# Attention and routed experts on one core: a planner's tie rule, where the row maxima are written, and the attention's end cut in parts

## The chip, the cores and the metric

The kernel runs on one core of one Trainium2 chip. The metric is the device time of one execution in microseconds (us): 815.42 us as the median of three runs before the change (815.18 to 823.71). One further execution was recorded by the profiler; it took 812.64 us.

## The reference

Eight batch elements with eight heads, 576 positions and head size 64. Attention has a causal mask and a bias from running sums, and its output goes, token by token, to one of eight experts with a capacity of 576 tokens each.

```python
scores = 1/sqrt(D) * q @ k.T
bias = -(cum[:, :, :, None] - cum[:, :, None, :])        # cum = cumsum(max(s, 0))
scores = where(causal, -1e9, scores + minimum(bias, 0))
attn = exp(scores - max(scores)); attn = attn / (sum(attn) + 1e-9)
x = (attn @ v) as [4608 tokens, 512]
logits = x @ w_gate                                      # [4608, 8]
for idx in argsort(-logits.flatten()):                   # best pair first
    tok, e = idx // 8, idx % 8
    if assigned[tok] < 0 and counts[e] < 576: assigned[tok] = e; counts[e] += 1
out[mask_e] = max(x[mask_e] @ w1[e], 0) @ w2[e]          # for each expert e
```

## The kernel before

**Two stages.** The attention (class `Attention`) writes x, split in two f16 halves, to a DRAM tensor `xs` and the logits to a tile `L`. Then `route_and_experts` finds the experts' tokens in eight phases (class `Router`) and runs the experts one after the other (class `Moe`): gather by token numbers, first product, relu, second product, scatter. Nearly all products are made from f16 parts (high and low), hence the many matmuls.

**A planner sets the order.** The kernel is scheduled by hand: `Plan.add` takes a task with its engine (t = PE, a = ACT, v = DVE, p = POOL, s = SP's DMA queue), an estimated duration, what it depends on, a priority, and the ring buffers that it uses. `Plan.run` simulates the engines when the kernel is built. In each step it takes for each engine the task that can start first (by priority among equals) and starts the one of these that can start earliest; equal times are decided by priority. The instructions are emitted in that order. On the chip each engine's queue is in order, so the plan decides what stands behind what; semaphores do the rest. A task with `lock=True` on DVE or POOL starts in the plan only when the other engine's last locked task is over: this is how the plan models the port to SBUF that DVE and POOL share. All of POOL's compute tasks are locked. A task with `alt` may go to a second engine.

**The attention.** One group g is half the heads of a batch element (16 groups), one pass is a pair of heads (two per group, 32 in all, n = 2g + pr). Per pass:

- `load` and `vload` (once per group) fetch q, k and v; ACT makes the high parts (L379, L412), DVE the low parts (L381 for q and k, L414 for v: `Vl`); SP moves halves between partitions (L386).
- `spass`: PE computes score tiles into one of three PSUM buffers `pss` (L473, L457), and DVE takes each row's maximum with one fused instruction, mask added (`tri`, L442). It writes its elementwise result to a buffer `scr`, of which there is one and which nobody reads, and the maximum to a column of `mr`. Ten of these per pass. The maxima are turned (L489 to L497) and go by DMA into rows of QK (L499, `mt`).
- `sts`: PE computes the transposed scores with the maximum subtracted into `pst` (L514 to L517, L556 to L558), ACT takes the exponential into P (L525), POOL subtracts P's bfloat16 high part from it (L527): R. Six R of 512 columns and one of 128 per pass.
- `pv`: three matmuls per tile pair into `po` (L587 to L589), five query tiles per head. `norm` divides by the row sum on DVE (L602 to L604), makes the high half of x on ACT (L606) and the low half on DVE (L608).
- `turn`: PE transposes the two halves (L635), ACT copies them to `xt` (L638), PE computes the logits' dots with `wgp` (L645), which `gate` made from w_gate (L304, L306). After a batch element DVE adds them up into L (L651).

After the fourth, seventh and eighth batch element `batch_tasks` runs `choose` (L815 to L827, eleven small DVE instructions: best expert, its key, its digit) on the columns that are new. `xout` writes x to `xs` at the end of each batch element (L616, L618).

**The router's first phase** compares the digits of all 40 columns with all thresholds (L906, `ge`), counts by matmul (L929, L939), and narrows in seven such steps. Its pools are opened after the attention's pools are closed and lie in the same memory.

## Time and profile before

| what | us |
|---|---|
| median of three runs | 815.42 |
| the profiled execution | 812.64 |
| its span on the core | 810.9 |
| PE busy, of the span | 726.9 (90%) |
| DVE busy | 607.9 (75%) |
| ACT busy | 379.6 (47%) |
| POOL busy | 345.6 (43%) |

PE is the matmul unit, PEld its weight load, DVE the vector engine, ACT the scalar engine, POOL GpSimd, SP the queue that issues most DMAs. L442 is line 442 of the kernel. A row of the timeline has the start and the duration in us, engine, line, operation, written and read tiles with their shapes, and in brackets how long the engine had been idle and for whom it waited. Matmul rows are pipelined: their starts are what counts. Shares over the whole span say little here, since the attention (to about 318 us), its tail, the first phase of the router (to about 395 us) and the experts have different limits.

### The profile page before, as it was taken

To read this page: it belongs to the slowest core of one execution; us is meant where nothing else is said; L and a number is where in the kernel's file an instruction comes from. 1 tells how busy PE (TensorE), PEld (TensorE's weight loads), DVE (VectorE), ACT (ScalarE), POOL (GpSimd) and SP (SyncE) were. 2 spreads that over 40 slices of the span, in tenths; PEclk is the share of its full clock that TensorE was granted. 3 is DMA by queue.
4 is the path that set the end of the run, shared out by engine and by line. 5 is a ranking of instruction groups with operands and counts; after the bars stand their busy time and mean duration, and the time that the engine had idled before them with its cause. 6 is when DMAs were issued, how large, how long until landed. Compare 5 with 4: busy or idle time off the path is not lost.

```text
span 810.9 us, 22772 instructions
## 1 busy us (share of the span) xinstructions
PE 726.9 (90%) x8814; PEld 459.3 (57%) x8814; DVE 607.9 (75%) x2070; ACT 379.6 (47%) x724; POOL 345.6 (43%) x425
## 2 busy tenths in 40 slices
PE   4188999999999999824899999999999999999995
PEld 1066788878778888712754545545445454454542
DVE  8768999999999997658888887887878888350110
ACT  3356788878778776602532333432234333341110
POOL 4268788787879887601105031130222114301111
PEclk8578999999999999955999999999999999999998
DMA  4956567686847431013438265393837548931001
GB/s 125 315 163 168 161 196 212 168 238 162 255 135 228 110 102 62 2 59 125 144 118 234 90 162 165 132 232 132 150 124 202 156 143 196 280 117 39 21 21 38
DMA packets 85315, 119.27 MB, mean 147 GB/s; under 512 B 40726, under 2 KB 57238, under 8 KB 85206
## 3 DMA queue, kind: packets, MB, share of 16 engines
q1 hardware_dynamic: 79318, 98.93, 43.3%
q0 software_dynamic: 5888, 18.88, 7.7%
q8 instruction: 69, 1.13, 0.6%
q14 instruction: 40, 0.33, 0.1%
HBM read 71.67 MB, written 19.10 MB: 112 GB/s over the span
## 4 chain that ended last, share of the span: by engine, by line
PE 58%; issue 18%; DVE 12%; DMA 5%; POOL 4%; SPq 1%; ACT 1%; POOLq 0%; another core or an unknown queue 0%; DVEq 0%; ACTq 0%
PE psm L1200 14%; PE psm L1274 13%; DVE scr L442 5%; PE pst L515 4%; PE pst L514 4%; PE pss L473 3%; PE po L587 3%; PE po L589 2%; PE po L588 2%; PE psm L1271 2%; PE psn L1204 2%; POOL out_dram L1254 2%; PE pss L635 1%; PE pss L457 1%; POOL xg L1134 1%
## 5 line engine op out<-in xcount | busy, mean ns | idle before, releaser
L527 POOL TENSOR_TENSOR R<-P 128x512 f16<-128x512 f32 (+1 forms) x224 | 232.8, 1066 | 50.8 <-ACT P L525 49.9
L1200 PE MATMUL psm<-xT,w1p 128*128 128x512 f16 (+1 forms) x876 | 194.1, 353 | 0.0
L1274 PE MATMUL psm<-w2p,hT 128*128 128x512 f16 x768 | 174.7, 379 | 0.0
L525 ACT ACTIVATE P<-pst 128x512 f32<-128x512 f32 (+1 forms) x224 | 119.0, 548 | 50.5 <-PE pst L517 23.2
L1204 PE MATMUL psn<-xT,w1p 128*128 128x64 f16 x768 | 142.2, 193 | 0.0
L442 DVE CUSTOM_DVE_ANT_0 scr<-pss,mS 128x512 bf16<-128x512 f32 (+3 forms) x256 | 124.7, 487 | 16.0 <-PE pss L473 6.4
L1200 PEld LDWEIGHTS <-w1p 128*128 128x128 f16 x876 | 79.7, 98 | 81.6 <-issue 1.4
L1134 POOL DMA_INDIRECT xg<-xs,ids x40 | 42.9, 1072 | 191.7 <-DVE val L824 52.9
L1254 POOL DMA_INDIRECT out_dram<-y,ids x40 | 41.5, 1037 | 183.7 <-ACT y L1285 156.9
L587 PE MATMUL po<-V,P 128*128 128x65 f16 x960 | 113.7, 196 | 2.4 <-DVE xp L608 2.0
L514 PE MATMUL pst<-QK 70*128 70x64 f16 (+4 forms) x512 | 109.0, 252 | 6.8 <-DMA QK<-mt 6.8
L1274 PEld LDWEIGHTS <-hT 128*128 128x128 f16 x768 | 69.0, 98 | 80.4 <-issue 4.0
L589 PE MATMUL po<-V,R 128*128 128x65 f16 x960 | 113.7, 194 | 0.1
L588 PE MATMUL po<-Vl,P 128*128 128x64 f16 x960 | 113.4, 193 | 0.0
L515 PE MATMUL pst<-QK 128*128 128x64 f16 (+4 forms) x512 | 107.6, 251 | 0.0
L1220 ACT ACTIVATE hT<-psm 128x512 f16<-128x512 f32 x64 | 38.2, 597 | 123.5 <-PE psm L1200 103.0
L588 PEld LDWEIGHTS <-P 128*128 128x128 bf16 x960 | 89.9, 99 | 7.8 <-issue 2.8
L587 PEld LDWEIGHTS <-P 128*128 128x128 bf16 x960 | 90.3, 98 | 5.8 <-issue 2.3
L473 PE MATMUL pss<-QK 67*128 67x512 f16 (+3 forms) x256 | 74.1, 311 | 17.6 <-DVE mr L442 10.1
L589 PEld LDWEIGHTS <-R 128*128 128x128 f16 x960 | 89.8, 97 | 0.3 <-POOL R L527 0.3
L1285 ACT ACTIVATE y<-psm 128x512 f32<-128x512 f32 x32 | 19.1, 597 | 122.7 <-PE psm L1274 105.2
L1204 PEld LDWEIGHTS <-w1p 128*128 128x128 f16 x768 | 72.8, 98 | 0.6
(210 smaller groups left out, 1394.1 us busy)
## 6 DMA issues: line engine op xcount, KB each, us to landing
QK<-QK SPq DMA_DIRECT2D x120, 144.0 KB
wst<-in_w_dram SPq DMA_DIRECT2D x32, 512.0 KB
wst<-in_w_dram SPq DMA_DIRECT2D x64, 256.0 KB
rv<-in_v_dram SPq DMA_DIRECT2D x16, 576.0 KB
raw<-in_q_dram SPq DMA_DIRECT2D x15, 576.0 KB
raw<-in_k_dram SPq DMA_DIRECT2D x15, 576.0 KB
xs<-xp SPq DMA_DIRECT2D x8, 1024.0 KB
xs<-xp SPq DMA_DIRECT2D x8, 128.0 KB
```

The costliest lines, as they stand in the source:

```text
L442: return pl.add("v", dur, lambda: nc.vector.tensor_tensor_reduce(scr.t[:, :n], ps(), mask, 1.0, init() if init else -3e38, OP.add, OP.max, ...
L473: nc.tensor.matmul(ps.t[:, :n], F()[:, q0:q0 + 128], F()[:, k0:k0 + n], start=True, stop=True)
L514: nc.tensor.matmul(ps[:, c0:c0 + n], F()[:, ks:ks + 128], F()[:, q:q + n], start=True, stop=False)
L515: nc.tensor.matmul(ps[:, c0:c0 + n], G()[:, ks:ks + 128], G()[:, q:q + n], start=False, stop=not diag)
L525: e = pl.add("a", n / 1200 + 0.171, lambda: nc.scalar.activation(P.t[:, c0:c0 + n], ps.t[:, :n], AF.Exp, scale=1.0 / YS), [x] + fresh, pri ...
L527: sub = lambda eng: eng.tensor_tensor(R.t[:, c0:c0 + n], P.t[:, c0:c0 + n], strided_hi(P.t)[:, c0:c0 + n], op=OP.subtract)
L587: nc.tensor.matmul(o[:, i], H[:, c:c + 128], V.t[:, pr, sl], start=f, stop=False)
L588: nc.tensor.matmul(o[:, i, 0:64], H[:, c:c + 128], Vl.t[:, pr, sl], start=False, stop=False)
L589: nc.tensor.matmul(o[:, i], R.t[:, c:c + 128], V.t[:, pr, sl], start=False, stop=l)
L1200: nc.tensor.matmul(ps[:, tiles[0]:tiles[-1] + 1] if len(tiles) > 1 else ps[:, tiles[0]], lhs(f, c, a), xT.t[:, tiles[0]:tiles[-1] + 1, 4 * ...
L1204: nc.tensor.matmul(pt.t[:, 64 * f:64 * f + 64], lhs(f, c, a), xT.t[:, 4, 4 * b + c, 0:64], start=s, stop=e)
L1274: nc.tensor.matmul(py.t, hT.t[:, f, a, 128 * i:128 * i + 128], w2p.t[:, f, b], start=f == 0 and k == 0, stop=f == 7 and k == 2)
```

## The change

- **Tie rule.** In `Plan.run`, tasks of different engines that can start at the same time are now compared first by the time since which task and engine have been waiting, and only then by priority. Two tasks that wait for the shared port fall under this.
- **Maxima.** `tri` writes its elementwise result back to the PSUM buffer that it read; `scr` is gone.
- **Sooner.** The two pieces of `gate` get priority -20 (before: 1), the low part of v 2g - 2 (before: 2g - 0.9).
- **Locks.** Nine of the eleven pieces of `choose` are locked in the plan. The batch after the seventh element has its priority number raised by 5 where it was 2.
- **End of the attention.** R of the last pass may go to DVE. The norm of the last head pair is made in two parts, tiles 0 to 2 and 3 to 4 (`parts`), as are the turn, the copies (the second may go to DVE) and the dots.
- **Router.** The last batch element's logits are no longer added up in the attention but in the first phase (`late`), with `choose` on its five columns, between the first eight tenths of the first `ge` and the rest; one reduce replaces two. The three pools of the router are opened with `reuse_waits="tile"`: a tile waits for the tiles that lay in its place, where before all waited for the closing of the old pools.

```diff
-                if best is None or (t, x.prio, x.rank) < best[:3]:
-                    best = (t, x.prio, x.rank, x, e)
+
+                z = (t, max(x.ready, self.free[e]), x.prio, x.rank, x, e)
+                if best is None or z[:4] < best[:4]:
+                    best = z
             assert best is not None, "no task can go on"
-            self.start(best[0], best[3], best[4])
+            self.start(best[0], best[4], best[5])
...
-            mt=R(w, [20, 128], F16, "mt", 2), scr=R(w, [128, 512], BF, "scr", 1, False),
+            mt=R(w, [20, 128], F16, "mt", 2),
...
         x = pl.add("v", 0.2, lambda: nc.vector.tensor_scalar(self.wgp[:, :, 0, :], self.wgf, GS, None, op0=OP.mult), [ld],
-                   prio=1, lock=True)
+                   prio=-20, lock=True)
         self.k["gate"] = pl.add("v", 0.2, lambda: nc.vector.scalar_tensor_tensor(
-            self.wgp[:, :, 1, :], self.wgf, GS, self.wgp[:, :, 0, :], op0=OP.mult, op1=OP.subtract), [x], prio=1, lock=True)
+            self.wgp[:, :, 1, :], self.wgf, GS, self.wgp[:, :, 0, :], op0=OP.mult, op1=OP.subtract), [x], prio=-20, lock=True)
...
-            Vl.t, rv.t, VS, V.t[:, :, :, 0:64], op0=OP.mult, op1=OP.subtract), [hi], prio=t0 - 0.9, uses=[rv, V, Vl], lock=True)
+            Vl.t, rv.t, VS, V.t[:, :, :, 0:64], op0=OP.mult, op1=OP.subtract), [hi], prio=t0 - 2, uses=[rv, V, Vl], lock=True)
...
-            scr = self.buf("scr")
             dur = n / 960 + 0.156 + (0.06 if init else 0)
             return pl.add("v", dur, lambda: nc.vector.tensor_tensor_reduce(
-                scr.t[:, :n], ps(), mask, 1.0, init() if init else -3e38, OP.add, OP.max, mr.t[:, o:o + 1]),
-                [dep] + list(more), prio=prio, uses=[ps.buf, scr, mr])
+                ps(), ps(), mask, 1.0, init() if init else -3e38, OP.add, OP.max, mr.t[:, o:o + 1]),
+                [dep] + list(more), prio=prio, uses=[ps.buf, mr])
...
-            r = pl.add("p", n / 547 + 0.1, lambda: sub(nc.gpsimd), [e] + fresh, prio=prio + 0.3, uses=[P, R])
+            r = pl.add("p", n / 547 + 0.1, lambda: sub(nc.gpsimd), [e] + fresh, prio=prio + 0.3, uses=[P, R], lock=True,
+                       alt=("v", n / 960 + 0.16, lambda: sub(nc.vector)) if n0 == 4 * self.nb - 1 else None)
...
+                xs_[i] = x
+            for a, z in self.parts(n0, par):
+                self.norm(g, pr, par, po, den, xp, xs_[z - 1], a, z)
+
+    def parts(self, n, par):
+
+        return ((0, 3), (3, 5)) if n == 4 * self.nb - 1 and par else ((0, 5),)
...
+        m = z - a
+        o = lambda: po.t[:, 0:325].rearrange("p (i c) -> p i c", c=65)[:, a:z]
...
+        lo = V(0.157 + m / 15, lambda: v.tensor_sub(xp.t[:, a:z, 1, h:h + 64], o()[:, :, 0:64], xp.t[:, a:z, 0, h:h + 64]), [hi], us=[xp])
+        self.xdone.setdefault(b, []).append((hi, lo, a, z))
...
+        for i0, i1 in self.parts(2 * g + pr, 1):
+            m, out = i1 - i0, []
+            need = [f for f in fin if f[2] < i1 and f[3] > i0]
+            for a in range(2):
+                ps = self.buf("pss")
+
+                def turn(a=a, ps=ps, i0=i0, m=m):
+                    for i in range(m):
+                        nc.tensor.transpose(ps.t.bitcast(F16)[:, 128 * i:128 * i + 128],
+                                            xp.t[:, i0 + i, a, 128 * c:128 * c + 128], self.ident16)
+                x = pl.add("t", 0.058 * m, turn, [f[a] for f in need] + [k["i16b"]], prio=prio, uses=[ps, xp])
+                cp = lambda e, a=a, ps=ps, i0=i0, i1=i1, m=m: e(
+                    xt.t[:, a, i0:i1].rearrange("p i c -> p (i c)"), ps.t.bitcast(F16)[:, 0:128 * m])
+                last = 2 * g + pr == 4 * self.nb - 1 and a
+                out.append(pl.add("a", 0.171 + m * 0.1067, lambda cp=cp: cp(lambda y, z: nc.scalar.activation(y, z, AF.Copy)), [x],
+                                  prio=prio, uses=[ps, xt], alt=("v", 0.157 + m * 0.1333, lambda cp=cp: cp(nc.vector.tensor_copy)) if last else None))
+
+            def dots(i0=i0, i1=i1):
+                for i in range(i0, i1):
+                    for a, w in ((0, 0), (0, 1), (1, 0)):
+                        nc.tensor.matmul(o[:, c, i], xt.t[:, a, i], self.wgp[:, c, w], start=(a, w) == (0, 0), stop=a == 1)
+            x = self.dots = pl.add("t", 0.088 * m, dots, out + [k["gate"], self.dots] + free, prio=prio + 0.5, uses=[xt])
...
+        add = lambda: nc.vector.tensor_reduce(self.L[:, 5 * b:5 * b + 5], o.rearrange("p k i e -> p i e k"), AX.X, OP.add)
+        if b == self.nb - 1:
+            self.router.late = add
+            return
+        self.lg[b] = ends = [pl.add("v", 0.33, add, [x, k["router"]], prio=prio + 1)]
         self.fresh_lg += ends
-        if b in (3, self.nb - 2, self.nb - 1):
-            b0 = {3: 0, self.nb - 2: 4}.get(b, b)
-            self.router.batch_tasks(pl, b0, b, self.fresh_lg, prio + 2)
+        if b in (3, self.nb - 2):
+            self.router.batch_tasks(pl, 0 if b == 3 else 4, b, self.fresh_lg, prio + (2 if b == 3 else 5))
...
-        P = lambda name, bufs, **k: ctx.enter_context(self.tc.tile_pool(name=name, bufs=bufs, **k))
+        P = lambda name, bufs, **k: ctx.enter_context(self.tc.tile_pool(name=name, bufs=bufs, reuse_waits="tile", **k))
...
+            x = pl.add("v", part(dur), f, list(deps) if n == 0 else [x], prio=prio + n / 100, lock=n not in (0, 5))
...
+        early = 0 if j else 8
...
+                def f_ge(q0=0, q1=NC_ // G, gt=gt, n=n, w_=w_):
+                    Bs = [128, q1 - q0, n, G]
+                    v.tensor_tensor(gt()[:, q0:q1], w_().rearrange("p (q c) -> p q c", c=G)[:, q0:q1, None].to_broadcast(Bs),
                                     form.kj[:, None, :n].to_broadcast(Bs), op=OP.is_ge)
-                g = V(0.155 + NC_ * n / 1920, f_ge, takes=[ge], uses=[wd] if wd else ())
+                if s == 0 and early:
+                    V(0.155 + early * G * n / 1920, lambda f_ge=f_ge: f_ge(0, early), takes=[ge])
+                    V(0.33, self.late)
+                    for dur, f in self.choose(slice(NC_ - 5, NC_)):
+                        V(0.15 + (dur - 0.15) / 8, f)
+                    g = V(0.155 + (NC_ - early * G) * n / 1920, lambda f_ge=f_ge: f_ge(early), uses=[ge])
+                else:
+                    g = V(0.155 + NC_ * n / 1920, f_ge, takes=[ge], uses=[wd] if wd else ())
```

More of the change, by code (lines that the diff above doesn't have):

```diff
@@ L571, in pv @@
             po, den = self.buf("po"), self.buf("den")
-            x = None
+            x, xs_ = None, {}
             for i in range(5):
@@ L627, in turn @@
         prio = 2 * g + pr + 2.6
-        xp, fin = self.xps[b], self.xdone[b][2 * c:2 * c + 2]
-        xt, out = self.buf("xt"), []
-        for a in range(2):
-            ps = self.buf("pss")
-            def turn(a=a, ps=ps):
-                for i in range(5):
-                    nc.tensor.transpose(ps.t.bitcast(F16)[:, 128 * i:128 * i + 128], xp.t[:, i, a, 128 * c:128 * c + 128],
-                                        self.ident16)
-            x = pl.add("t", 0.29, turn, [f[a] for f in fin] + [k["i16b"]], prio=prio, uses=[ps, xp])
-            out.append(pl.add("a", 0.7, lambda a=a, ps=ps: nc.scalar.activation(
-                xt.t[:, a].rearrange("p i c -> p (i c)"), ps.t.bitcast(F16)[:, 0:640], AF.Copy), [x], prio=prio, uses=[ps, xt]))
+        xp, fin = self.xps[b], self.xdone[b][2 * c:]
@@ L640, in turn @@
+        xt = self.buf("xt")
         o = self.r["po"].slots[b % 2][0][:, 340:500].rearrange("p (k i e) -> p k i e", k=4, i=5)
-        def dots():
-            for i in range(5):
-                for a, w in ((0, 0), (0, 1), (1, 0)):
-                    nc.tensor.matmul(o[:, c, i], xt.t[:, a, i], self.wgp[:, c, w], start=(a, w) == (0, 0), stop=a == 1)
         free = self.lg.get(b - 2, []) if c == 0 else []
-        x = self.dots = pl.add("t", 0.44, dots, out + [k["gate"], self.dots] + free, prio=prio + 0.5, uses=[xt])
+        for i0, i1 in self.parts(2 * g + pr, 1):
[18 more added lines that the diff above has]
+            x = self.dots = pl.add("t", 0.088 * m, dots, out + [k["gate"], self.dots] + free, prio=prio + 0.5, uses=[xt])
@@ L648, in turn @@
         if c < 3:
             return
-        last = b == self.nb - 1
-        self.lg[b] = ends = [pl.add("v", 0.3, lambda n=n, s=s: nc.vector.tensor_reduce(
-            self.L[:n, 5 * b + s.start:5 * b + s.stop], o[:n, :, s].rearrange("p k i e -> p i e k"), AX.X, OP.add),
-            [x, k["router"]], prio=prio + 1) for n, s in ((128, slice(0, 4)), (64, slice(4, 5)))]
+        add = lambda: nc.vector.tensor_reduce(self.L[:, 5 * b:5 * b + 5], o.rearrange("p k i e -> p i e k"), AX.X, OP.add)
```

20 lines of the change are left out of this document (6 added, 14 removed).

## The prediction, made before the change was run

> **What bounds the kernel now.** I read the busy times by stage first (start and end, then PE, PEld, DVE, ACT and POOL busy, granted clock, DMA share, GB/s).
>
> ```profile
> 41.60:80.00 38.40, 34.84 (x454) 25.32 (x454) 30.05 (x102) 23.10 (x48) 28.20 (x35) 0.80 0.62 168
> 80.00:318.00 238.00, 233.06 (x4522) 190.64 (x4520) 224.72 (x795) 186.06 (x402) 196.28 (x209) 1.00 0.59 168
> 318.00:351.00 33.00, 24.50 (x579) 21.55 (x575) 17.71 (x59) 18.17 (x37) 18.17 (x20) 0.94 0.21 74
> 395.00:811.00 416.00, 400.44 (x2987) 203.97 (x2985) 271.31 (x907) 128.05 (x208) 82.31 (x116) 0.99 0.49 137
> ```
>
> From 395 us on the experts keep PE busy 96% of the time, and the change edits none of that work: whatever is won or lost before 395 us moves the end by the same amount. So the question is the attention (to 318 us), its tail (318 to 351 us) and the first step of the router. In the attention PE is busy 233.06 of 238 us and DVE 224.72. PE's idle 4.9 us understate its waits, because a matmul's row lasts 0.19 us while the next may start 0.03 us later. Here is one wait in the order of time on PE:
>
> ```profile
> 191.08 0.19 PE L588 MATMUL po<-Vl,P 128*128 128x64 f16 x1
> 191.11 0.19 PE L589 MATMUL po<-V,R 128*128 128x65 f16 x1
> 191.65 0.32 PE L473 MATMUL pss<-QK 67*128 67x384 f16 x1 [0.34 <-DVE mr L442]
> ...
> PE pss L473 <- DVE mr L442: 1.7, 3, 1.2
> PE pss L457 <- DVE mr L442: 2.4, 1, 2.4
> ```
>
> A 64-column matmul takes a slot of 0.03 us; the score matmul at 191.65 starts 0.54 us after its predecessor, 0.51 us late. Going through all matmul starts between 80 and 318 us in this way (columns at 0.03 us per 64), 57 starts are over 0.04 us late and together 12.6 us; what releases them is DVE: a free pss buffer, a norm piece. (The last two rows are the list of waits, for 80 to 318 us and for 41.6 to 80 us: total, times, longest.) So PE is the bound with 12.6 us of gaps, and these come from DVE, which itself has little left.
>
> Why DVE has little left shows in its own order of time:
>
> ```profile
> 203.52 0.08 DVE L442 DVE_READ_ACCUMULATOR2_ANT mr<- 128x1 f32 x1
> 203.52 0.18 DVE L603 RECIPROCAL den<-den 128x5 f32<-128x5 f32 x1
> 203.75 0.69 DVE L442 CUSTOM_DVE_ANT_0 scr<-pss,mS 128x512 bf16<-128x512 f32 x1
> ...
> 206.37 0.08 DVE L442 DVE_READ_ACCUMULATOR2_ANT mr<- 128x1 f32 x1
> 206.37 0.49 DVE L608 TENSOR_TENSOR xp<-po,xp 128x320 f16<-128x320 f32 x1
> 206.77 0.68 DVE L442 CUSTOM_DVE_ANT_0 scr<-pss,mS 128x512 bf16<-128x512 f32 x1
> 207.38 0.08 DVE L442 DVE_READ_ACCUMULATOR2_ANT mr<- 128x1 f32 x1
> 207.61 0.75 DVE L442 CUSTOM_DVE_ANT_0 scr<-pss,mZ,mr 128x512 bf16<-128x512 f32 x1
> ...
> L442 DVE DVE_READ_ACCUMULATOR2_ANT mr<- 128x1 f32 x264 | 21.7, 82 | 0.0
> ...
> L442 DVE CUSTOM_DVE_ANT_0 scr<-pss,mS 128x128 bf16<-128x128 f32 x52 | 14.9, 287 | 1.6
> ```
>
> A maximum is the L442 pass with its accumulator read. Any other instruction starts with that read (L608 at 206.37), a further maximum 0.23 us after it (207.38 to 207.61), and behind a short reciprocal still 0.23 us after the read. All maxima write the one scr buffer, so each waits until the one before is complete.
>
> Third, the port that DVE and POOL share. L527 (R on POOL), L381 and L414 (low parts of q, k, v on DVE) in 80 to 318 us:
>
> ```profile
> L527 POOL TENSOR_TENSOR R<-P 128x512 f16<-128x512 f32 x156 | 180.1, 1177 | 35.0 <-ACT P L525 34.4
> L381 DVE SCALAR_TENSOR_TENSOR QK<-raw,QK 128x1152 f16<-128x1152 f32 x24 | 33.7, 1420 | 0.0
> L414 DVE SCALAR_TENSOR_TENSOR Vl<-rv,V 128x1152 f16<-128x1152 f32 x13 | 17.8, 1366 | 0.0
> ```
>
> An undisturbed R takes 1.04 us (the x9 row below: 7.75 us for seven large and two small ones), its mean is 1.18 us, so about 156 x 0.14 = 21 us of POOL is blocked time. Taken one after the other, 156 R at 1.04 and the two DVE groups are 214 us, with the 128-column R some 223 of 238: the port has about 6% left.
>
> **The change, part by part.** *Maxima in place.* The result goes back to pss instead of scr; the instruction count stays. Does writing PSUM cost more? L604 writes po in PSUM and L608 writes SBUF, both 320 columns: 0.49 us each, so I take 0. The wait on scr goes: of the 264 maxima, 47 stand directly behind a read and lose 0.205 us on average, 36 behind a reciprocal 0.125, 34 behind a tensor_scalar 0.076, together 9.6 + 4.5 + 2.6 = 16.7 us of DVE. The pair on one pss buffer (L442 over 384 and over 64 columns) may keep its wait, once per pass. DVE then needs about 7% less, PE becomes the bound, and the most that can come out is PE's 12.6 us of waits, 2.2 of which I count under the batch. The lower end is 0 (the order of PE's queue is fixed by the planner, and a wait removed may show at the next slot), the upper 10.3. With the port at 94% and DVE near 92% of a shorter stage I take half: **5.2 us**.
>
> The Trainium skill, on its page VectorE: DVE Perf Modes, section "The DRAIN you can't avoid", says that chaining operations without semaphores gains nothing, the flush between them being paid anyway. By that rule this term would be 0. The rows above disagree: 0.23 us with the wait against a start together with the read without one.
>
> *The router's batches.* After the fourth batch element (near 230 us) and the seventh (near 325 us) eleven small DVE instructions run. They read two SBUF operands or run wide, and beside an R they take the length of an R:
>
> ```profile
> 230.78 1.00 DVE L825 TENSOR_SCALAR dg<-sg 128x20 int32<-128x20 int32 x1
> ...
> 325.47 0.91 DVE L816 TENSOR_TENSOR eq<-L,m 128x120 f32<-128x120 f32 x1
> ...
> 347.78 0.20 DVE L816 TENSOR_TENSOR eq<-L,m 128x40 f32<-128x40 f32 x1
> 348.62 0.16 DVE L825 TENSOR_SCALAR dg<-sg 128x5 int32<-128x5 int32 x1
> ```
>
> The change marks nine of the eleven as needing the port, and puts the second batch behind the norms in priority. Around 230 us two PE waits of 0.86 and 1.32 us follow the batch: bounds 0 to 2.2, I take **1.5**. In the tail PE's PV waits 1.78 us, until 331.10 (row below), for an L608 queued behind the batch. Bounds 0 to 1.8; nine pieces of some 0.2 us now hold POOL back between R's, 1.8 us of POOL which the R moved to DVE partly return, so I take **1.2**.
>
> *Port to the one that waits longer, v's low part sooner.* These reorder only. V's low part is early already:
>
> ```profile
> 304.79 1.55 DVE L414 SCALAR_TENSOR_TENSOR Vl<-rv,V 128x1152 f16<-128x1152 f32 x1
> ...
> 331.10 0.19 PE L587 MATMUL po<-V,P 128*128 128x65 f16 x1 [1.78 <-DVE xp L608]
> ...
> PE pst L514 <- DMA QK<-mt: 6.8, 1, 6.8
> ```
>
> The last L414 ends at 306.3, its first PV matmul is at 331.1 us, so moving it forward buys nothing on PE and puts 1.35 us ahead of some maxima. What covers those is the lead of the maxima over their use: PE waited for the mt transfer once, at 41.65 us (last row), and never between 80 and 318 us. I take 0, bounds -4 and +3. Without that lead each of the 13 L414 would cost up to 1.35 us.
>
> *Gate sooner.* Its two pieces go from 53 us into the first microseconds of DVE's queue, in front of the first low parts of q and k. They cost twice 0.18 us there if they lie on the path (their first row below has 0.51 us, blocked). Where they stood:
>
> ```profile
> 53.17 0.51 DVE L304 TENSOR_SCALAR wgp<-wgf 128x32 f16<-128x32 f32 x1
> ...
> 60.32 2.24 DVE L381 SCALAR_TENSOR_TENSOR QK<-raw,QK 128x1152 f16<-128x1152 f32 x1
> ```
>
> Between 41.6 and 80 us the starts that wait for DVE are 4.7 us late, most of it the 2.4 us wait listed above, behind the blocked L381 (2.24 us against 1.35). Shorter maxima, no gate pieces and a better turn at the port should win part; the SP queue's new order at the start can win or lose more than that. Bounds -2 and +4, I take **2.0**.
>
> *R of the last pass on DVE or POOL.* An R is 0.69 us on DVE by the maximum of 512 columns (an estimate from that row), 1.04 on POOL. The Trainium skill, page SBUF — State Buffer, section "Who interferes with whom", holds that a DVE instruction with two SBUF inputs excludes a GpSimd instruction that reads SBUF. By that rule the two don't run side by side, and the trace agrees: 0.91 us for an L816 that alone takes 0.20.
>
> So a moved R saves 0.35 us, not 1.04: three of seven make 1.0 us of POOL. PE works nearly through in that stretch, so I take **0.5**, bounds 0 and 1.0.
>
> *The end in parts, and the router's entry.* Rows of the tail:
>
> ```profile
> 332.28 7.75 POOL L527 TENSOR_TENSOR R<-P 128x512 f16<-128x512 f32 x9 [2.89 <-ACT P L525]
> ...
> 342.36 0.17 DVE L602 TENSOR_SCALAR den<-po 128x5 f32<-128x5 f32 x1 [1.01 <-PE po L589]
> 343.00 0.49 DVE L608 TENSOR_TENSOR xp<-po,xp 128x320 f16<-128x320 f32 x1 [0.48 <-PE po L645]
> 343.41 0.18 DVE L603 RECIPROCAL den<-den 128x5 f32<-128x5 f32 x1
> ...
> 347.13 0.38 DVE L651 TENSOR_REDUCE L<-po 128x32 f32<-128x128 f32 x2 [1.95 <-PE po L645]
> ...
> 348.86 0.16 DVE L827 CAST w<-dg 128x5 bf16<-128x5 int32 x1
> 350.27 0.82 DVE L906 TENSOR_TENSOR ge<-w,kj 128x1280 f16<-128x1280 bf16 x1 [1.25 <-DMA xs<-xp]
> ...
> 344.22 0.44 ACT L606 ACTIVATE xp<-po 128x320 f16<-128x320 f32 x1 [1.89 <-DVE po L604]
> 345.26 1.30 ACT L638 ACTIVATE xt<-pss 128x640 f16<-128x640 f16 x2 [0.61 <-PE pss L635]
> ```
>
> From the last PV to the logits (342.36 to 347.13) the chain of one norm, turn, copy and dots is 4.8 us. The last piece now has two of five tiles. Its L604 and L608 lose 192 columns each, at about 1.03 ns (estimated from L442: 0.68 us at 512 columns, 0.29 at 128) 0.2 us each. On ACT a copy of 640 columns is 0.65 us and one of 320 is 0.44, 0.7 ns per column: 0.13 off L606 and 0.27 off the one L638 on the path. Fewer transposes and dots give some 0.4. That is 1.2, and the 0.48 us for which L608 waited may go too; the first part's added instructions lie beside the last PV. I take **1.5**, bounds 1.0 and 2.2. At the router, L906 stood 1.25 us for the xs write, since a pool gave up its memory as a whole; now each tile waits for what lay under it. And 4/5 of L906 run before the last logits: 0.82 falls to about 0.3 on the path. That is 1.25 + 0.5 = 1.75, plus 0.05 for one reduce instead of two: **1.8**, bounds 1.2 (small waits per tile) and 2.3.
>
> **Sum.** 5.2 + 1.5 + 1.2 + 2.0 + 0.5 + 1.5 + 1.8 = 13.7 us. The profiled execution took 812.64 us (span 810.9 and 1.7 around it), which gives 798.9. The median of the three timed runs, 815.42, lies 2.8 us above it, so the forecast for the median is **801.7 us**. The terms' bounds added up run from a loss of 4 us to a gain of 27.
>
> **Rivals.** *Only the tail gains.* The 57 late starts are set by the order of PE's queue and only move, or the maxima keep a wait of their own on the DVE (the pair on one buffer, or the mr columns). The rule on the DRAIN would give this result too. For it: twelve microseconds in 57 places, none over 1.4, look like rough edges of an order, not like one wait. Against it: nearly all are released by DVE. Worth 5.0 us of the tail and 1 of the batch: 809.4.
>
> *PE runs through.* With maxima lasting what the planner supposes, plan and chip agree and nearly all waits go: 10.3 + 2.2 + 3 + 6 = 21.5 us, 793.9. Against it speaks the port at 94%.
>
> *Slower, by the port.* The rule of the longer wait is settled in the planner's time. If on the chip a DVE piece reaches the head of its queue in the middle of an R, all of DVE stands behind it, as at 60.32 us (0.9 us lost). There are 37 such pieces in 80 to 318 us, and DVE has 13.3 us idle there. At 0.85 us each they cost 31.5 - 13.3 = 18 us; less 5 in the tail this is 828. It decides from about 0.7 us per piece on. Against it: now their means are only 0.07 and 0.02 us over an undisturbed 1.35, so the planner's times fit well.
>
> **How the numbers follow.** Forecast 0.57, only the tail 0.17, PE through 0.17, the port 0.09. The range 791 to 812 takes in the first three with some width and leaves the slow case out. Something over 1% (8.2 us) can be told from no change. The forecast's own spread is some 797 to 807, all but a little of it faster by over 1%; the tail case is within 1%, the port case mostly slower: 0.75, 0.17, 0.08.
>
> **What would show it.** Right: maxima that start together with the read before them; 57 late starts reduced to half their 12.6 us, PE still the busiest; L816 to L827 at 0.2 to 0.3 us; no 1.78 us wait of PV in the tail; L906 no longer waiting for the xs write; the experts' stage as long as before. Wrong: maxima still 0.2 us behind each other; L381 and L414 well over 1.4 us; a longer way to the first score matmul at 41.65 us; a second stage that isn't simply shifted.

## The result and the profile after

The kernel after takes 809.30 us as the median of six runs (805.08 to 812.16), the kernel before 819.36 in the runs made beside it: a ratio of 0.989, interval 0.986 to 0.993. The profiled execution took 809.16 us, its span is 807.2. By that ratio the gain is 8.7 us (the two medians lie 10.1 apart) where 13.7 were forecast, and 809.30 is 6.1 us below the 815.42 from which the forecast counted. The time lies in the range, and the gain is not made of the parts that the forecast named.

Busy time by stage of the kernel after (start and end, length, then PE, PEld, DVE, ACT and POOL busy, granted clock, DMA share, GB/s):

```profile
15.00:41.60 26.60, 17.56 (x83) 7.89 (x82) 25.18 (x71) 11.02 (x19) 9.21 (x10) 0.50 0.87 276
41.60:80.00 38.40, 34.91 (x546) 26.62 (x547) 32.71 (x111) 25.03 (x51) 27.91 (x36) 0.86 0.47 126
80.00:318.00 238.00, 233.04 (x4527) 191.21 (x4526) 227.00 (x767) 186.66 (x398) 202.01 (x208) 1.00 0.62 180
318.00:351.00 33.00, 20.91 (x480) 17.65 (x477) 22.85 (x88) 13.09 (x29) 9.41 (x11) 0.80 0.11 38
395.00:811.00 416.00, 393.81 (x2775) 195.24 (x2772) 261.11 (x880) 122.74 (x200) 81.84 (x116) 0.98 0.48 134
```

From 80 to 318 us PE has 4527 matmuls and 233.04 us busy; before, it had 4522 and 233.06. The attention's steady stage has become no faster. What is new stands ahead of it, 83 matmuls from 15 to 41.6 us against 22, and 546 from there to 80 us against 454, so that less is left for the tail (480 against 579 from 318 to 351 us). Before, the first of these stretches read:

```profile
15.00:41.60 26.60, 6.94 (x22) 2.35 (x23) 19.43 (x48) 7.46 (x9) 8.91 (x22) 0.50 0.98 285
```

The last row of the table above can't be set against its counterpart before (400.44 us of PE, 2987 matmuls): the kernel after has begun its experts 10 us earlier and ends at 807.2, so less of them falls between 395 and 811 us. To put all this on one scale I add up the columns of the matmuls from 15 us on at the slot of 0.03 us per 64 that the prediction used (unrounded 0.0267; a matmul of fewer columns counts as 64), and take the times of three marks:

| profile | PE columns done by 80 us | by 318 us | last PV matmul | first expert matmul | from there to the last w2 matmul |
|---|---|---|---|---|---|
| before | 27.3 | 237.9 | 342.12 | 392.13 | 409.1 |
| after | 34.6 | 244.4 | 333.59 | 381.66 | 415.9 |

The lead is 7.3 us at 80 us, 6.5 at 318, 8.5 at the last PV and 10.5 at the first expert matmul. The experts then give 6.8 of it back, in a stage whose instructions are the same and stand in the same order on every engine. The medians, 8.7 to 10.1 us apart, do not show this loss; it belongs to the two profiled executions.

The wait that the maxima had is gone, in DVE's order of time after:

```profile
206.32 0.41 DVE L443 CUSTOM_DVE_ANT_0 pss<-pss,mS 128x256 f32<-128x256 f32 x1
206.66 0.13 DVE L443 DVE_READ_ACCUMULATOR2_ANT mr<- 128x1 f32 x1
206.66 0.72 DVE L443 CUSTOM_DVE_ANT_0 pss<-pss,mS 128x512 f32<-128x512 f32 x1
207.31 0.13 DVE L443 DVE_READ_ACCUMULATOR2_ANT mr<- 128x1 f32 x1
207.31 0.15 DVE L611 TENSOR_SCALAR den<-po 128x5 f32<-128x5 f32 x1
207.39 2.20 DVE L416 SCALAR_TENSOR_TENSOR Vl<-rv,V 128x1152 f16<-128x1152 f32 x1
```

At 206.66 a maximum starts together with the read in front of it, where before 0.23 us lay between. The last row shows what waits now: v's low part takes 2.20 us in place of 1.35, most likely behind an R on the shared port. The groups of 80 to 318 us (count, busy us, mean ns, idle before):

```profile
L383 DVE SCALAR_TENSOR_TENSOR QK<-raw,QK 128x1152 f16<-128x1152 f32 x24 | 36.0, 1499 | 0.0
L443 DVE DVE_READ_ACCUMULATOR2_ANT mr<- 128x1 f32 x251 | 34.9, 139 | 0.0
L613 DVE TENSOR_TENSOR po<-po,den 128x320 f32<-128x320 f32 x52 | 26.9, 518 | 0.9 <-PE po L661 0.5
L416 DVE SCALAR_TENSOR_TENSOR Vl<-rv,V 128x1152 f16<-128x1152 f32 x14 | 21.2, 1511 | 0.0
```

The read takes 139 ns against 82, L383 1499 against 1420, L416 1511 against 1366. PE's late starts from 80 us to the last three passes add up to 13.0 us; counted in the same way they were 12.1 before (from 80 to 318 us, as in the prediction, 13.2 against 12.6).

The start shows in the first `mt` transfer on SP's queue and in the first transposed scores, which wait for it, before and after:

```profile
36.36 0.70 SPq L499 DMA_DIRECT2D QK<-mt  x1
41.65 0.58 PE L514 MATMUL pst<-QK 70*128 70x512 f16 x1 [6.79 <-DMA QK<-mt]
```

```profile
22.64 0.72 SPq L500 DMA_DIRECT2D QK<-mt  x1
27.86 0.59 PE L515 MATMUL pst<-QK 70*128 70x512 f16 x1 [0.68 <-DMA QK<-mt]
```

The end of the attention on DVE, after:

```profile
329.33 0.69 DVE L528 TENSOR_TENSOR R<-P 128x512 f16<-128x512 f32 x1 [0.59 <-ACT P L526]
...
336.71 0.36 DVE L652 COPY xt<-pss 128x384 f16<-128x384 f16 x1 [0.22 <-PE pss L649]
336.98 0.68 DVE L923 TENSOR_TENSOR ge<-w,kj 128x1024 f16<-128x1024 bf16 x1
337.69 0.32 DVE L665 TENSOR_REDUCE L<-po 128x40 f32<-128x160 f32 x1
...
339.56 0.29 DVE L923 TENSOR_TENSOR ge<-w,kj 128x256 f16<-128x256 bf16 x1
```

The first piece of `ge` (L923) runs without a wait, and an R on DVE takes the 0.69 us that were estimated. The batch after the seventh element has lost nearly all of its blocked time; the piece that took 0.91 us in the prediction's row, with the same shape, now reads:

```profile
318.08 0.27 DVE L831 TENSOR_TENSOR eq<-L,m 128x120 f32<-128x120 f32 x1
320.56 0.72 DVE L833 TENSOR_SCALAR m<-m 128x15 f32<-128x15 f32 x1
```

All others of this batch take 0.16 to 0.28 us; L833 is the only one over that.

### The profile page after: what moved, and what is told of

Its sections match the earlier page's. It is cut to its first block, busy times and chain, and to the rows that moved or that the text cites. A ratio compares the mean times of both kernels' runs of the same rounds, so it can differ in the third digit from the quotient of the medians.

```text
span 807.2 us, 22538 instructions
## 1 busy us (share of the span) xinstructions
PE 735.1 (91%) x8814; PEld 461.5 (57%) x8814; DVE 613.7 (76%) x2067; ACT 380.2 (47%) x726; POOL 347.3 (43%) x426
## 4 chain that ended last, share of the span: by engine, by line
PE 57%; issue 17%; DVE 16%; DMA 3%; POOL 3%; ACT 1%; SPq 0%; another core or an unknown queue 0%; POOLq 0%; DVEq 0%; ACTq 0%
PE psm L1224 14%; PE psm L1298 13%; DVE pss L443 5%; PE pst L515 4%; PE pst L516 4%; PE pss L474 3%; PE po L589 3%; DVE QK L383 2%; PE po L591 2%; PE po L590 2%; PE psm L1295 2%; PE psn L1228 2%; PE pss L649 2%; POOL out_dram L1278 2%; POOL xg L1158 1%
## 5 line engine op out<-in xcount | busy, mean ns | idle before, releaser
L528 POOL TENSOR_TENSOR R<-P 128x512 f16<-128x512 f32 (+1 forms) x221 | 233.5, 1080 | 35.2 <-ACT P L526 33.7
L1298 PE MATMUL psm<-w2p,hT 128*128 128x512 f16 x768 | 177.8, 384 | 0.0
L443 DVE CUSTOM_DVE_ANT_0 pss<-pss,mS 128x512 f32<-128x512 f32 (+3 forms) x256 | 123.6, 499 | 7.1 <-PE pss L474 4.5
L589 PE MATMUL po<-V,P 128*128 128x65 f16 x960 | 115.6, 196 | 1.0 <-DVE xp L617 0.7
L591 PE MATMUL po<-V,R 128*128 128x65 f16 x960 | 115.7, 194 | 0.0
L590 PE MATMUL po<-Vl,P 128*128 128x64 f16 x960 | 115.3, 193 | 0.0
L474 PE MATMUL pss<-QK 67*128 67x512 f16 (+3 forms) x256 | 77.1, 319 | 11.9 <-DMA QK<-xp 5.2
```

What stands on the lines that cost most here:

```text
L443: return pl.add("v", dur, lambda: nc.vector.tensor_tensor_reduce(ps(), ps(), mask, 1.0, init() if init else -3e38, OP.add, OP.max, mr.t[:, ...
L474: nc.tensor.matmul(ps.t[:, :n], F()[:, q0:q0 + 128], F()[:, k0:k0 + n], start=True, stop=True)
L528: sub = lambda eng: eng.tensor_tensor(R.t[:, c0:c0 + n], P.t[:, c0:c0 + n], strided_hi(P.t)[:, c0:c0 + n], op=OP.subtract)
L589: nc.tensor.matmul(o[:, i], H[:, c:c + 128], V.t[:, pr, sl], start=f, stop=False)
L590: nc.tensor.matmul(o[:, i, 0:64], H[:, c:c + 128], Vl.t[:, pr, sl], start=False, stop=False)
L591: nc.tensor.matmul(o[:, i], R.t[:, c:c + 128], V.t[:, pr, sl], start=False, stop=l)
```

## The experiments

The theories at the outset. **A, the order:** the planner's order for the kernel before already hid the wait on `scr`; what the edit gains at one place PE waits for at another, and the new order would lose without the edit. **B, the price:** the gain is there, and is eaten by writing PSUM and by the port. **C, for the experts:** the loss of 6.8 us comes from the execution or the chip, and not from the change; its rival is that the pools' new places in memory do it.

All kernels in one table, profiles and ratios against the kernel before on the same chip; "steady" is PE columns between 80 and 318 us, "late" the late starts as above:

| kernel | by 80 us | steady | late | last PV | first expert matmul | experts | ratio and interval |
|---|---|---|---|---|---|---|---|
| rep_before | 27.3 | 210.6 | 12.1 | 342.06 | 392.82 | 402.6 | 0.999 (0.997 to 1.001) |
| rep_after | 34.1 | 209.5 | 13.1 | 334.50 | 383.07 | 403.0 | 0.984 (0.981 to 0.987) |
| one_scr | 33.4 | 194.1 | 31.6 | 352.55 | 400.76 | 404.4 | 1.010 (1.006 to 1.014) |
| three_scr | 35.4 | 211.3 | 11.0 | 331.10 | 378.80 | 404.3 | 0.979 (0.975 to 0.983) |
| scr_planned | 27.0 | 197.9 | 26.5 | 355.98 | 403.64 | 404.9 | 1.011 (1.007 to 1.016) |
| old_tie | 34.7 | 206.7 | 16.4 | 336.79 | 385.20 | 403.2 | 0.989 (0.987 to 0.992) |
| before_tie | 32.6 | 198.6 | 23.8 | 350.00 | 400.41 | 402.8 | 1.008 (1.005 to 1.012) |
| before_inplace | 30.7 | 209.2 | 13.7 | 339.94 | 390.69 | 403.3 | 0.998 (0.996 to 1.000) |
| hop_before | 24.3 | 190.9 | 34.0 | 369.90 | 420.42 | 403.1 | 1.031 (1.025 to 1.036) |
| not_sooner | 37.3 | 209.4 | 13.0 | 331.06 | 378.14 | 403.8 | 0.985 (0.980 to 0.990) |
| whole_pools | 35.2 | 212.3 | 10.5 | 330.22 | 383.61 | 403.5 | 0.989 (0.983 to 0.994) |
| whole_end | 35.4 | 211.7 | 11.2 | 330.64 | 378.98 | 403.2 | 0.981 (0.976 to 0.986) |
| hop35_before | 29.9 | 196.9 | 26.5 | 355.54 | 405.86 | 410.4 | 1.016 (1.011 to 1.021) |
| hop_after | 34.4 | 207.5 | 16.2 | 336.64 | 384.41 | 410.7 | 0.992 (0.989 to 0.994) |
| half_R | 34.4 | 214.9 | 7.2 | 328.27 | 375.85 | 412.8 | 0.984 (0.979 to 0.989) |
| three_whole | 35.0 | 215.9 | 6.9 | 326.59 | 374.73 | 410.9 | 0.978 (0.974 to 0.983) |
| after_again | 35.6 | 212.9 | 10.2 | 329.31 | 376.50 | 402.6 | 0.984 (0.982 to 0.987) |
| three_again | 35.6 | 214.6 | 8.3 | 327.43 | 374.88 | 404.5 | 0.979 (0.976 to 0.981) |

**The two kernels again, side by side on another chip.**

> The kernel before, profiled once more. The experts' stage (first to last expert matmul) took 409.1 us in the first profile of before and 415.9 us in that of after, with the same order of instructions on every engine. Theory A (chance: PE waits for the router's small matmuls, and a wait of some 2 us sets its clock back): the stage comes out anywhere from 408 to 418 us, other than 409.1 by over 2 us. Theory B (the shift itself makes the stage longer): 409 again within 1 us. By both the attention's stage repeats: last PV near 342 us, first expert matmul near 392 us, within 1 us.

> The changed kernel, profiled once more. Theory A (chance): the experts' stage is other than 415.9 us by over 2 us. Theory B: 416 us again within 1 us. By both the attention repeats: first score matmul with maxima at 27.9 us, last PV near 333.6 us, first expert matmul near 381.7 us, within 1 us.

The experts take 402.6 and 403.0 us, the first less than the 408 to 418 that theory A had: the loss of 6.8 is not the change's, and C holds. On this chip the gain is 11.6 us at the median (808.53 to 796.94), nearly all of it ahead of the experts (9.8). In the table four chips have experts of 402.6 to 404.9 us and a fifth (hop35_before, hop_after, half_R, three_whole) 410.4 to 412.8, whichever kernel it is.

**One buffer back, three buffers, in the order of after.** The instructions stay in the order of the kernel after; only where the elementwise result goes changes, to one `scr` buffer in SBUF (the wait is back) or to three in turn (no wait, no writing of PSUM).

```diff
+        self.scrs = [w.tile([128, 512], BF, name=f"scr{i}") for i in range(1)]   # three_scr: range(3)
...
-                ps(), ps(), mask, 1.0, init() if init else -3e38, OP.add, OP.max, mr.t[:, o:o + 1]),
+                self.scrs[next(self.nscr) % 1][:, :n], ps(), mask, 1.0, init() if init else -3e38, OP.add, OP.max, mr.t[:, o:o + 1]),
```

> The changed kernel with its plan and order of instructions kept, but each maximum writes its elementwise result to one scr buffer in SBUF again, so the wait of each maximum for the one before it is back. My prediction's theory (the wait costs 16.7 us of DVE in the steady stage, half of it shows): last PV 4 to 9 us later than in the changed kernel, at 338 to 343 us. Rival (writing into PSUM costs DVE as much as the wait did: accumulator reads are 0.139 us after the change, 0.082 before): last PV within 1.5 us of 333.6.

> The changed kernel with its plan and order kept, but the maxima write in turn to three scr buffers in SBUF: neither the wait nor the write into PSUM. If writing into PSUM costs some 0.045 us per maximum (251 of them in the steady stage, 11 us of DVE), accumulator reads are back at 0.08 us and the last PV comes 2 to 5 us earlier, at 329 to 332 us, and the whole kernel is faster by as much. If PE or the shared port is the bound anyway, and DVE's time doesn't matter: last PV at 333.6 within 1 us.

DVE with one buffer, and the list of PE's waits from 80 to 318 us (total, times, longest):

```profile
206.24 0.08 DVE L446 DVE_READ_ACCUMULATOR2_ANT mr<- 128x1 f32 x1
206.44 0.49 DVE L620 TENSOR_TENSOR xp<-po,xp 128x320 f16<-128x320 f32 x1
207.05 0.69 DVE L446 CUSTOM_DVE_ANT_0 scr<-pss,mS 128x512 bf16<-128x512 f32 x1
207.67 0.08 DVE L446 DVE_READ_ACCUMULATOR2_ANT mr<- 128x1 f32 x1
207.67 2.16 DVE L386 SCALAR_TENSOR_TENSOR QK<-raw,QK 128x1152 f16<-128x1152 f32 x1
```

```profile
PE pss L477 <- DVE mr L446: 5.1, 16, 0.6
PE po L592 <- DVE xp L620: 4.4, 8, 0.8
PE pss L652 <- DVE mr L446: 3.1, 7, 0.7
```

In after's order the wait costs 18.1 us by the last PV (352.55 against 334.50), where 4 to 9 were expected, and more than the 16.7 us of DVE that the prediction counted. A likely reason, not tested by itself, is that it meets a DVE that is full and a port that is fuller: L386 has a mean of 1.66 us where after has 1.53 on this chip. By the rule of the Trainium skill, page VectorE: DVE Perf Modes, section "The DRAIN you can't avoid", which rests on eight copies timed with and without semaphores between them, this experiment would show nothing; the runs disagree for a maximum that waits for the one before.

With three buffers the last PV comes 3.4 us sooner than with the result in PSUM, and 21.5 sooner than with one buffer, from which it differs only in the number of buffers. The reads and the norm's product, in 80 to 318 us:

```profile
L616 DVE TENSOR_TENSOR po<-po,den 128x320 f32<-128x320 f32 x53 | 26.2, 495 | 1.0 <-PE po L664 0.5
...
L446 DVE DVE_READ_ACCUMULATOR2_ANT mr<- 128x1 f32 x251 | 20.4, 81 | 0.0
```

81 ns against 139, and 495 against 518: writing the result back to PSUM is what lengthened the read (there it is f32, in `scr` bf16; the place and the type were not tried apart). So B is true as well, but small: 3.5 us at the median here (796.94 to 793.40), against the 18 of the wait.

**The plan knows of one buffer; the tie rule taken out; the tie rule alone; in place alone.**

```diff
# scr_planned: after, with the old tri
+            scr = self.buf("scr")
-                [dep] + list(more), prio=prio, uses=[ps.buf, mr])
+                [dep] + list(more), prio=prio, uses=[ps.buf, scr, mr])
# old_tie: after, with
-                z = (t, max(x.ready, self.free[e]), x.prio, x.rank, x, e)
+                z = (t, x.prio, x.rank, x.rank, x, e)
# before_tie: before, with the first line; before_inplace: before, with
-                scr.t[:, :n], ps(), mask, 1.0, init() if init else -3e38, OP.add, OP.max, mr.t[:, o:o + 1]),
+                ps(), ps(), mask, 1.0, init() if init else -3e38, OP.add, OP.max, mr.t[:, o:o + 1]),
```

> The changed kernel with the one scr buffer back in SBUF, the planner told of it as before (all of the change but the maxima's edit). With the changed plan left as it was, the same wait cost 18 us (last PV at 352.6 instead of 334). Theory A (the wait itself is the cost): last PV 345 to 353 us, the kernel 10 to 18 us slower than the changed one. Theory B (a plan that knows of the wait puts other work between the maxima, as the kernel before did): last PV 336 to 342 us, 3 to 8 us slower than the changed one.

> The kernel before with the new tie rule alone. If that rule makes the lead at the start: 32 to 35 us of PE column time done by 80 us instead of 27.3. If it is the rule that slows the steady stage: 5th to 29th pass 224 to 230 us instead of 220.7, so that the whole comes out within 1% of before. If it does neither, all as before.

> The changed kernel with the old tie rule (priority alone). PE has done 34 us of column time by 80 us in the changed kernel, 27 before. If the tie rule makes this lead (its SP queue issues the first mt transfer as the 20th DMA instead of the 30th): lead down to 0 to 4 us here (the 24th), and in exchange a steady stage (5th to 29th pass) back from 224.6 to 217 to 221 us, since L381 and Vl wait less for the port. If the tie rule is not the cause of the slower steady stage: 224 us again, and the kernel slower than the changed one by the lost lead.

> The kernel before with the maxima written back to PSUM alone (planned so). My prediction's term: half of PE's 10.3 us of waits in the steady stage, 5th to 29th pass from 220.7 to some 215 us, and the kernel 5 to 8 us faster. Rival (the plan had hidden the wait already, and the write into PSUM costs what the wait did): 219 to 222 us, and only the earlier first mt transfer (24th DMA instead of 30th) is left, 0 to 3 us faster.

The whole change without its maxima edit is 1.1% slower than before, and the tie rule alone 0.8%. In place alone, planned anew, is worth 0.2%, with a steady stage of 209.2 us: the same as after's 209.8, the same as before's 210.6. So the edit that pays in one order buys next to nothing in the other. This is the rival of its expectation, which has two halves: the plan had hidden the wait, and the write into PSUM costs what is left of it. The run does not tell them apart; the kernel before with three buffers in its own order was not run. In the column "steady" two families stand apart: every order with the wait has 191 to 199 us, every order without it 207 to 216, and only the kernel before has 210.6 in spite of the wait. Taking the tie rule out of after costs some 4 us if its 0.989 is set against the 0.984 that after has on two other chips (on the first it had 0.989 too); on its own chip after was not timed. Its expectation failed in both halves: the lead at 80 us stays (34.7) and the steady stage is slower (206.7).

**Is the order of before an exception?** `HOP` is the time that the planner supposes from the end of a task to the start of one that waits for it on another engine. A hundredth of a microsecond in it gives another order of the same tasks.

```diff
-    HOP = 0.04
+    HOP = 0.05   # hop_before, hop_after; hop35_before: 0.035
```

> The kernel before with one number of the planner's model changed (the hop between engines 0.05 us instead of 0.04): no instruction added or taken away, only the order worked out anew. In 80 to 318 us PE did 210.6 us of column time in the kernel before; edits that re-plan it left 198 to 209. Theory A (before's order is one of the best of many near ones, and any edit of the planner draws a new one): 197 to 208 us here, the kernel 3 to 12 us slower. Theory B (orders differ little, and the tie rule or the maxima made the difference): 209 to 212, the same time within 3 us.

> The kernel before, order worked out anew with a hop of 0.035 us instead of 0.04. If before's order is a good draw and a usual one with the wait on scr does 190 to 199 us of PE columns between 80 and 318 us (as four others did): 190 to 200, 10 to 26 us slower. If a hop of 0.05 was a bad draw by itself and before is usual: 205 to 211, within 6 us of before.

> The changed kernel, order worked out anew with a hop of 0.05 us, the number that cost the kernel before 26 us. If the maxima without a wait leave DVE enough room for a usual order: 206 to 212 us of PE columns between 80 and 318 us, the kernel within 5 us of the changed one. If the changed kernel's order is a good draw too: under 203, over 8 us slower.

The kernel before loses 3.1% and 1.6% by it, the first more than even theory A had expected, the kernel after (0.992, on a chip where it was not itself timed) less than 1%. PV matmuls between 80 and 318 us tell it at one glance, before, before with another order, after, and after with one buffer:

```profile
L587 PE MATMUL po<-V,P 128*128 128x65 f16 x775 | 91.3, 195 | 0.6 <-DVE xp L608 0.3
```

```profile
L587 PE MATMUL po<-V,P 128*128 128x65 f16 x705 | 83.0, 197 | 0.7 <-DVE xp L608 0.7
```

```profile
L589 PE MATMUL po<-V,P 128*128 128x65 f16 x785 | 95.0, 195 | 0.9 <-DVE xp L617 0.7
```

```profile
L592 PE MATMUL po<-V,P 128*128 128x65 f16 x715 | 86.0, 195 | 4.9 <-DVE xp L620 4.4
```

Of 775 matmuls 705 remain when before's order is drawn anew. The first half of A is what these runs show: the order of before was a lucky one among those with the wait. Three orders with HOP at 0.035, 0.04 and 0.05 are not a distribution, and how rare it is stays open.

**What holds the steady stage at 210 us?** In half_R POOL's R is made on half its columns from the third pass on, which takes POOL's busy time from 202 to 130 us in that stage and changes no order.

```diff
-            sub = lambda eng: eng.tensor_tensor(R.t[:, c0:c0 + n], P.t[:, c0:c0 + n], strided_hi(P.t)[:, c0:c0 + n],
+            m_ = n if n0 < 2 else n // 2
+            sub = lambda eng: eng.tensor_tensor(R.t[:, c0:c0 + m_], P.t[:, c0:c0 + m_], strided_hi(P.t)[:, c0:c0 + m_],
```

> The changed kernel in its own order, but from the third pass on POOL's subtraction covers only the first half of its columns (the other half of R keeps older values, so part of the low half of P is left out). It frees some 70 us of POOL and of the shared port between 80 and 318 us and no DVE work. If the port is what bounds the steady stage: L383 and Vl back to 1.35 us, PE's waits from 11 to 13 us down to under 4, the last PV 8 us or more earlier than 334 us. If DVE's own work or PE's order is the bound: PE's waits stay over 8 us, the last PV within 4 us.

All that is left on PE's list of waits, 80 to 318 us:

```profile
PE pss L474 <- DVE mr L443: 0.4, 2, 0.2
PE pst L515 <- DMA QK<-QK: 0.2, 1, 0.2
PE pss L496 <- POOL mp L494: 0.2, 1, 0.2
```

Late starts fall to 7.2 us, L383 is back at 1404 ns and L416 at 1381, and the last PV comes at 328.27. The kernel after itself varies, though: in its three profiles late starts are 10.2 to 13.1 us, L383 takes 1397 to 1532 ns, the last PV comes between 329.31 and 334.50, while before's two stand 0.1 us apart. So the port's load can be worth 1 to 6 us, and this run doesn't tell it from a shorter R on POOL, since both come with it. Its late starts and its last PV lie between what the two theories had expected. That the port is the next bound is likely and not shown.

**The other parts of the change, each taken out of after.**

```diff
# not_sooner: gate's prio=-20 back to 1 (twice), Vl's prio=t0 - 2 back to t0 - 0.9
# whole_pools
-        ... self.tc.tile_pool(name=name, bufs=bufs, reuse_waits="tile", **k))
+        ... self.tc.tile_pool(name=name, bufs=bufs, **k))
# whole_end
-        return ((0, 3), (3, 5)) if n == 4 * self.nb - 1 and par else ((0, 5),)
+        return ((0, 5),)
```

> The changed kernel with the priorities of the gate's pieces and of v's low part as before. If these make the lead at the start: 28 to 31 us of PE column time by 80 us instead of 34.4. If the tie rule makes it (the first mt transfer is again the 20th DMA): 33 to 35. For the whole: my prediction gave the gate a part of 2 us and v's low part nothing, so 0 to 3 us slower than the changed kernel; by theory A of the new order drawn, anything from -2 to 10 us slower.

> The changed kernel with the router's pools waiting as a whole again; the plan and the order are unchanged, only waits come back. Prediction: from the last PV to the first expert matmul 1.25 us (bounds 0.7 to 1.8) longer than the changed kernel's 48.1 to 48.6; since the early part of the first comparison can't start before the xs write has landed either, up to 2.5 us. Rival (the wait for the pool is hidden behind the last logits now): no difference.

> The changed kernel with the last norm, turn, copies and dots in one part. The order up to the last pass is nearly the same. Prediction: from the last PV to the first expert matmul 1.2 us longer (bounds 0.7 to 2.0) than the changed kernel's 48.1 to 48.6. Rival (the added instructions of the first part cost what the shorter last part saves): within 0.4 us.

Gate and v sooner are worth nothing: 37.3 us of columns by 80 us without them, more than either theory had. The end in parts is worth little: from the last PV to the first expert matmul 48.3 us without it; with it 48.1, 48.6 and 47.2 in after's three profiles. On one chip the kernels without it are 0.3 to 1.3 us longer there (whole_end against not_sooner, three_again against after_again, three_whole against hop_after and half_R), but these pairs differ in other things too. The router's pools are worth 5 us, where at most 2.5 had been expected: without the tiles' own waits that stretch is 53.4 us, and DVE shows why:

```profile
339.71 0.69 DVE L923 TENSOR_TENSOR ge<-w,kj 128x1024 f16<-128x1024 bf16 x1 [6.00 <-DMA xs<-xp]
340.32 0.32 DVE L665 TENSOR_REDUCE L<-po 128x40 f32<-128x160 f32 x1
```

The early `ge` now stands ahead of the last reduce and of `choose`, and all of them wait 6.00 us behind it for the xs write.

**The best of the parts together.** Three buffers in SBUF and the end in one part, and the same beside the kernel after.

```diff
# three_whole, three_again: after with the edits of three_scr and of whole_end
```

> The changed kernel with three scr buffers in SBUF instead of the write into PSUM, and with the end in one part (the two parts gave nothing, the write into PSUM cost 3.5 us on one chip). Expected 1.9 to 2.4% faster than before, the changed kernel being 1.4 to 1.6% faster. If the write into PSUM costs nothing and the difference was the chip's: 1.5%.

> The changed kernel a third time, on the same chip as three_again. Expected 1.0 to 1.6% faster than before; last PV between 330 and 335 us.

> Three scr buffers in SBUF and the end in one part, on the same chip as after_again. If the write into PSUM costs DVE 0.045 us per maximum: 3 to 7 us faster than after_again, last PV 326 to 331 us. If not: within 2 us of it.

On one chip the kernel after takes 796.66 us (790.76 to 801.05) and this version 792.04 (790.64 to 795.91): 0.984 (0.982 to 0.987) and 0.979 (0.976 to 0.981) against the same runs of before. With three_scr, at 0.979, it is the fastest here. Its profiled execution has the last PV 1.9 us sooner than that of after, but experts that are 1.9 us longer, so that the medians alone speak for it in time.

## Why the prediction was right or wrong

**The maxima, 5.2 us: wrong, and this is the step that failed.** The mechanism on DVE came as foretold: a maximum starts with the read. What failed is the sentence that takes half of PE's 12.6 us of late starts. It assumed that these come from DVE having little left and would shrink with it. Measured are 210.6 to 209.8 us of columns and 12.1 to 13.0 us of late starts. The old order does as many columns with the wait as the new one without it, and a new plan of the old kernel without the wait gained 0.2% (before_inplace). In the new order it would have cost 18 us (one_scr). The edit pays for the new order and leaves no surplus. Its lower bound, 0, was the answer. How much of the missing 5.2 us the order took and how much the price of writing PSUM stays open: with neither wait nor price, in the new order, the steady stage does 211.3 us and late starts are 11.0, beside 210.6 and 12.1 of before on that chip (three_scr), but 214.6 and 215.9 us and 8.3 and 6.9 in executions on two other chips (three_again, three_whole), where before was not profiled.

**No price for writing PSUM: wrong.** The two rows that stood for it, L604 and L608, take 0.49 us each, and neither has an accumulator read behind it. The read went from 82 to 139 ns; three buffers get back 3.4 us by the last PV on the same chip, part of which may be the spread of after's own executions.

**Gate and start, 2.0 us: too small, and for another reason.** 7.3 us of lead at 80 us, not from gate (not_sooner) but with another order of SP's queue: the first `mt` transfer, the 46th DMA that SP issues before, is the 28th now. (The expectations count rows of the timeline, in which neighbouring DMAs of one line are one: about 30 and 20.) The prediction had seen that this order "can win or lose more than that" and gave it bounds of -2 and +4. Tie rule alone moves it to the 30th place, in place alone to the 36th, and both give a part (32.6 and 30.7 us by 80 us); scr_planned has it at the 39th and gains nothing there (27.0). The place alone does not settle it, for old_tie has it at the 36th as well and does 34.7 us. So it is another draw of the planner, and not the merit of one edit; what in the order makes the lead stays open.

**The total: luck.** At the start 5.3 us more than forecast, beyond that term's bound, stand against 6.0 us less in the steady stage.

**The batches.** The eleven pieces of the first one lie spread from 214.6 to 275.1 us now; nine take 0.14 to 0.37 us, about as foretold, two still 0.93 and 0.97 beside an R. What that is worth can't be told apart in a stage that as a whole lost 0.8 us. **Tail and R on DVE, 1.2 + 0.5:** the lead grows from 6.5 to 8.5 us, the pieces of the second batch are short, and no PV matmul waits any more; this fits, though no run takes these parts out. The 0.20 us that the prediction gives for an L816 alone belongs to a tile of a third of the size; unblocked, the same size takes the 0.27 us shown above.

**End in parts and the router's entry, 1.5 + 1.8:** 1.9 us on the first chip (50.0 to 48.1 from the last PV to the first expert matmul) and 2.2 on the second. The parts gave between nothing and 1.3, so the entry gave most of it; and its pools protect against 5 us rather than 1.25, since the early `ge` has put a wait for xs ahead of the logits.

**Tie rule and v's low part, 0:** within bounds as a sum, though the tie rule has two faces: 0.8% slower alone, some 4 us better with the rest (across chips).

**The experts as long as before:** true of the kernels on one chip (402.6 and 403.0), not of the first pair of profiles.

**The rivals.** "Only the tail gains" comes nearest: its reason, that a wait removed only moves the late starts, is what the steady stage shows. It left out the start, and that its 809.4 meets the 809.30 is luck: it counts from 815.42, where the six runs of before have 819.36. "PE runs through" did not come: 13 us of late starts remain, beside a DVE busy 227 of 238 us. "Slower, by the port" has its mechanism in L416 at 2.20 us, at means of +0.08 and +0.15 us instead of 0.7.

## What to carry to other kernels

In a kernel whose order is planned, a wait in the trace is no measure of what its removal brings: draw the order anew with a tiny change of a supposed time, with and without the wait, and compare the families. Count what a removed wait protects as well as what it saves; here 0.2% in a plan of the old kernel and 2.6% in the new one, both with the price of the write to PSUM in them. And the wait on a buffer that nobody reads was cheaper to end with two more buffers than with a write to PSUM, by 3.5 us.

## What the hardware showed beside this

**After two short waits PE's clock falls for some three microseconds.** In the experts of after's first profile:

```profile
472.84 0.19 PE L972 MATMUL psb<-ca,same 128*128 128x64 f16 x1 [1.68 <-DVE ca L969]
472.87 1.24 PE L1298 MATMUL psm<-w2p,hT 128*128 128x512 f16 x5
474.53 0.17 PE L978 MATMUL psb<-pe,share 128*128 128x8 f16 x1 [0.42 <-DVE pe L977]
474.55 3.14 PE L1298 MATMUL psm<-w2p,hT 128*128 128x512 f16 x7
```

Five matmuls of 512 columns take 1.24 us, seven a little later 3.14: 0.45 us each instead of 0.25. Busy time between 475 and 480 us of the same profile gives the granted clock, the last figure but two, as 0.70:

```profile
475.00:480.00 5.00, 5.00 (x24) 2.19 (x23) 3.41 (x11) 0.60 (x1) 1.15 (x2) 0.70 1.17 254
```

The Trainium skill, page TensorE: Matmul & The Clock Gate, Part 1, has two states of the clock in its table, half and full, and a window of about 3.4 us in which the activity is judged; the duration of the fall agrees. The page lets the clock fall after an idle window; here PE had stood for 1.68 and 0.42 us with work between. Before had a longer wait without a fall, so the length of one wait does not decide it:

```profile
484.21 0.17 PE L954 MATMUL psb<-pe,share 128*128 128x8 f16 x1 [1.76 <-DVE pe L953]
```

The clock records tell more. In every trace all changes of the granted clock lie on a grid of 3.41 us. Within the experts' stage of all profiles here it fell after the four windows of this grid in which PE had stood for 1.97 to 2.08 us in sum (two in after, one each in half_R and three_whole), and after none with 1.82 or less. Before's wait lay across two windows, of which one came to 1.36 us and the other to 0.65.

The same thing at 573.6 us and longer waits for the router's small matmuls make up the experts' difference: late starts there, with those behind a matmul at half clock, are 11.3 us in before's profile and 18.0 in after's, 6.7 of the 6.8. In the second pair they are 4.7 and 5.1. Why one chip or execution has 403 us and another 410 to 416 the runs don't tell.
